# Attention with two MoE layers on one core: the reciprocal of the row sums goes from VectorE to GpSimd, as a power of -1

## The chip, the core and the metric

The kernel runs on one core of a Trainium2 chip. The core has TensorE (matrix products, PE in the profile; its weight loads are PEld), VectorE (DVE), ScalarE (ACT), GpSimd (POOL) and SyncE (SP, which here starts the transfers). The engines run their own lists of instructions in order and wait for each other at semaphores. The metric is the device time of one execution in microseconds, the lower the better.

## The reference

The input is q, k and v of 4 batches, 8 heads, 576 positions and 64 numbers a head. The attention drops the scores that lie more than tau under the maximum of their row:

```python
scores = scale * np.matmul(q, k.transpose(0, 1, 3, 2))
thresh = np.max(scores, axis=-1, keepdims=True) - tau
scores = np.where(scores >= thresh, scores, -1000000000.0)
scores = scores - np.max(scores, axis=-1, keepdims=True)
attn = np.exp(scores)
attn = attn / (np.sum(attn, axis=-1, keepdims=True) + 1e-09)
return np.matmul(attn, v).astype(np.float32)
```

Its output, 2304 tokens of 512 numbers, goes through a first MoE, `(relu(x @ w_in) ** 2) @ w_out` with 2048 inner units, and then a second one: each token picks the expert with the largest of 8 gate logits, goes through `relu(x @ w1[e]) @ w2[e]` and is scaled by a gate.

## The kernel before

Two heads make a pair; a batch has 4 pairs, all batches together 16. Each pair has 9 chunks of 128 rows of queries (the last rows of both heads share a chunk), 144 chunks in all, 36 a batch. For a chunk these steps follow each other, with the line of each:

- TensorE makes the scores of 128 rows and 576 keys in PSUM (L612; L648 for the first four chunks).
- VectorE takes the negated maximum of a row (L615).
- ScalarE makes the exponential (L618), and meanwhile GpSimd the row's threshold (L623).
- VectorE zeroes what lies under the threshold and adds up the row (L627, "mask"; a second record reads the accumulated sum).
- GpSimd adds 1e-9 to the sum (L632), VectorE takes the reciprocal (L635).
- The row is scaled by it, "norm": on GpSimd (L638), for the first head of each pair in the first batch on ScalarE (L671).
- TensorE turns the 128 x 576 probabilities in five transposes (L680) into the one PSUM buffer that there is for it, and ScalarE copies them out (L688).

When a group of chunks is through, TensorE multiplies them with V (L707), and ScalarE and VectorE split the result in a high and a low part (L711, L714). The queries and keys of the next pair are split the same way ahead of time (L534 to L543). In the first batch there are three PSUM buffers for scores, shared with the product with V, and later two. Five buffers hold probabilities, four each the maxima, thresholds and sums.

As soon as a batch's attention is done, its first product of the first MoE (L771) runs between the chunks of the next batch; its weights are unpacked and split on ScalarE, VectorE and GpSimd (L746 to L756). After the attention come the second product (L889), the gate, and the second MoE's slots of tokens (L1155, L1205).

The order on each engine is made on the host before the kernel is built: every step is a task with an engine, an assumed duration and a priority; a list scheduler picks, engine by engine, the startable task with the smallest priority. A step's priority in the attention is the chunk's number plus an offset from the table `PLACE`, which has one number for the first batch and one for the others.

Of the kernel before, what the change touches and what calls it, by code (L numbers as in the profile page):

```python
# [9 lines left out]
F32 = mybir.dt.float32  # L10
# [5 lines left out]
ALU = mybir.AluOpType  # L16
# [199 lines left out]
def c_dve(n, rate=1):  # L216
    return n / 960 / rate + 0.068
# [40 lines left out]
def moa(ctx, tc, q, k, v, tau, w_in, w_out, wg, wog, w1, w2, ctab, coln, out):  # L258
    nc = tc.nc
    B, H, S, D = 4, 8, 576, 64  # L260
    P = 128
# [45 lines left out]
    const = ctx.enter_context(tc.tile_pool(name="const", bufs=1))  # L307
# [4 lines left out]
    g = Graph()  # L312


    PLACE = {
        "scores": (-9, -4),
        "max": (-16, 3),
        "exp": (4, -9),
        "bound": (-22, 3),
        "mask": (-11, -14),  # L320
        "sum": (-16, -13),
        "norm": (-3, 13),
        "turn": (-1, 8),
        "parts": (2, 9),
        "av": (2, 3),
        "prep": (6, 9),
        "x": (14, 11),
    }

    def K(nm, pr):  # L330
        return PLACE[nm][pr >= NP]
# [142 lines left out]
    nc.scalar.dma_start(taub, tau.rearrange("(o t) -> o t", o=1).broadcast_to([P, 1]))  # L474
    ntau = const.tile([P, 1], F32, name="ntau")
    nc.vector.tensor_scalar(ntau, taub, 0.0, -1.0, op0=ALU.max, op1=ALU.mult)
    qsc = const.tile([P, 1], F32, name="qsc")
    nc.vector.tensor_scalar(qsc, taub, 0.0, 0.125, op0=ALU.is_ge, op1=ALU.mult)

# [9 lines left out]
    def new(nm, tag):  # L489
        return Buf(ALL[nm], f"{nm}{tag}")  # L490
# [100 lines left out]
    def t_chunk(n, key):  # L591
        pr, st = divmod(n, NST)
# [3 lines left out]
        nm, th, sm = (new(x, n) for x in ("nm", "th", "sm"))  # L596
# [31 lines left out]
                p3, s.t[:, :, :HALF], th.t, p3, op0=ALU.is_ge, op1=ALU.mult, accum_out=sm.t  # L628
            )

        def r1():
            nc.gpsimd.tensor_scalar(sm.t, sm.t, 1.0, 1e-9, op0=ALU.mult, op1=ALU.add)  # L632

        def r2():
            nc.vector.reciprocal(sm.t, sm.t)  # L635

        def nrm():
            nc.gpsimd.tensor_scalar(p.t[:, :S], p.t[:, :S], sm.t, 1.0, op0=ALU.mult, op1=ALU.mult)  # L638
# [25 lines left out]
        g.add("ACT", c_act(S, True, 1), ex, [s, nm], [p], key + K("exp", pr))  # L664
        g.add("POOL", 0.2, thr, [nm], [th], key + K("bound", pr))
        g.add("DVE", c_dve(S) + 0.085, msk, [s, th], [p, sm], key + K("mask", pr))
        g.add("POOL", 0.2, r1, [], [sm], key + K("sum", pr))
        g.add("DVE", 0.09, r2, [], [sm], key + K("sum", pr))
        if pr < NP and hd == 0:
            g.add("ACT", c_act(S, False, 1),  # L670
                  lambda: nc.scalar.activation(p.t[:, :S], p.t[:, :S], AF.Copy, scale=sm.t), [sm], [p],  # L671
# [565 lines left out]
    for pr in range(NPR):  # L1237
        b, hp = divmod(pr, NP)
        if pr + 1 < NPR:
            pair_prep(pr + 1, (pr * NST + K("prep", pr)) * T0)  # L1240
        for st in range(NST):
            n = pr * NST + st
            t_chunk(n, n * T0)
            if st in READY:
                t_av(pr, READY[st], (n + K("av", pr)) * T0)
        if hp == NP - 1:
            if b == 1:
                for i in range(NFC):
                    t_w(i, wkey[i])
                for u in range(2 * NFC):  # L1250
                    t_h(0, u // 2, u % 2, (NP * NST + 8 + u * 1.125) * T0)
            for u in range(2 * NFC) if b else ():
                t_h(b, u // 2, u % 2, ((b + 1) * NP * NST + 8 + u * (1.125 if b < B - 1 else 0.25)) * T0)
# [109 lines left out]
```

## Time and profile before

| | us |
|---|---|
| median of 3 timed runs | 985.02 (983.87 to 986.71) |
| profiled execution | 990.66 |
| its span, first to last instruction | 988.9 |
| TensorE busy | 957.8 (97%) |
| VectorE busy | 613.1 (62%) |
| ScalarE busy | 595.5 (60%) |
| GpSimd busy | 278.8 (28%) |

The profiled execution is one run with the profiler on. Busy shares are averages over stages that differ: the attention of the first batch up to about 100 us, the attention of the other three with the first product of the first MoE between it up to about 430 us, and the rest. Columns of the views are named where they first stand. A record of a matmul is longer than the time to the next one, because they overlap. A wait is put down to the instruction that released it last by the profile: where the table names a reciprocal as what ScalarE or GpSimd waited for, it is often the instruction just before it that they need.

### The profile page before, as it was taken

How to read it: one execution, taken by the hardware profiler on the slowest of the kernel's cores; microseconds unless marked ns; L12 is line 12 of the kernel's file. 1: busy time of each engine (PE TensorE's matmuls, PEld its weight loads, DVE VectorE, ACT ScalarE, POOL GpSimd, SP SyncE). 2: the span in 40 equal slices, each digit the busy share in tenths (PEclk: the TensorE clock that was granted, in tenths of full speed). 3: DMA queues.
4: the chain of work that ended last, by engine and by line, in shares of the span. 5: the costliest groups of instructions: out<-in, count | busy, mean ns of one | idle time of the engine just before them, and what ended most of it. 6: DMA issues, size and time to landing. Idle time of an engine off the chain costs nothing. (4 is left out here: it accounts for less than half of the span.)

```text
span 988.9 us, 18351 instructions
## 1 busy us (share of the span) xinstructions
PE 957.8 (97%) x6194; PEld 829.9 (84%) x6194; DVE 613.1 (62%) x1414; ACT 595.5 (60%) x1122; POOL 278.8 (28%) x511
## 2 busy tenths in 40 slices
PE   8888999999999999999999999999999999999996
PEld 7665888898889888989988888887889989889885
DVE  6786898775666565657613444445877667777730
ACT  5787777776666665665324444444647667876731
POOL 3343676663343434410001000001114210211200
PEclk7998999999999999999999999999999999999999
DMA  6566758665555542469713444445949767877700
GB/s 161 143 166 171 205 165 236 185 177 146 148 135 149 131 116 82 128 196 281 219 55 108 107 107 107 107 107 131 265 128 334 263 219 265 299 263 252 269 21 25
DMA packets 130569, 167.42 MB, mean 169 GB/s; under 512 B 21279, under 2 KB 87327, under 8 KB 130466
## 3 DMA queue, kind: packets, MB, share of 16 engines
q1 hardware_dynamic: 126226, 155.63, 54.1%
q0 software_dynamic: 4096, 10.52, 3.4%
q8 instruction: 51, 0.84, 0.4%
q14 instruction: 52, 0.43, 0.2%
q10 hardware_dynamic: 144, 0.00, 0.0%
HBM read 110.33 MB, written 29.56 MB: 141 GB/s over the span
## 5 line engine op out<-in xcount | busy, mean ns | idle before, releaser
L889 PE MATMUL banks<-w,memr 128*128 128x512 f32 x648 | 158.4, 395 | 0.0
L627 DVE SCALAR_TENSOR_TENSOR memf<-banks,memf 128x576 f32<-128x576 f32 x144 | 116.1, 813 | 62.0 <-ACT memf L618 53.1
L771 PE MATMUL banks<-memr,w 128*128 128x288 f32 x960 | 140.9, 297 | 0.0
L618 ACT ACTIVATE memf<-banks,memf 128x576 f32<-128x576 f32 x144 | 105.6, 743 | 56.4 <-DVE memf L615 28.7
L889 PEld LDWEIGHTS banks<-w,memr 128*128 128x128 f32 x648 | 119.1, 188 | 23.8
L771 PEld LDWEIGHTS banks<-memr,w 128*128 128x128 f32 x960 | 130.8, 188 | 2.9 <-issue 2.9
L615 DVE TENSOR_REDUCE memf<-banks 128x1 f32<-128x576 f32 x144 | 107.1, 752 | 19.2 <-PE banks L612 14.5
L680 PE MATMUL banks<-ident,memf 128*128 128x128 f32 x720 | 105.8, 278 | 10.4 <-ACT pt L688 10.0
L612 PE MATMUL banks<-memr 128*128 128x288 f32 x592 | 110.2, 314 | 4.2 <-DVE memf L627 3.0
L688 ACT ACTIVATE pt<-banks 128x640 f32<-128x640 f32 (+1 forms) x160 | 102.7, 651 | 16.3 <-PE banks L680 12.0
L638 POOL TENSOR_SCALAR memf<-memf 128x576 f32<-128x576 f32 x128 | 103.7, 812 | 17.3 <-DVE memf L635 13.6
L680 PEld LDWEIGHTS banks<-ident,memf 128*128 128x128 f32 x720 | 83.9, 142 | 21.0 <-ACT pt L688 5.8
L994 POOL DMA_INDIRECT lst<-memf x18 | 18.7, 1039 | 273.6 <-DVE memf L980 209.3
L612 PEld LDWEIGHTS banks<-memr 128*128 128x128 f32 x592 | 84.1, 192 | 11.5 <-DVE memf L627 5.1
L707 PE MATMUL banks<-pt,memf 128*64 128x256 f32 (+1 forms) x640 | 89.3, 423 | 1.6 <-DVE memf L627 0.7
L874 DVE TENSOR_TENSOR memr<-memf,memr 128x512 fp32r<-128x512 f32 x72 | 47.7, 690 | 65.9 <-ACT memf L871 65.9
L1155 PE MATMUL banks<-memr,w 128*128 128x256 f32 x432 | 85.8, 284 | 2.0 <-DVE memr L1165 2.0
L1140 DVE TENSOR_TENSOR w<-memf,w 128x512 fp32r<-128x512 f32 x114 | 75.0, 688 | 20.2 <-ACT w L1137 19.0
L771 PE MATMUL banks<-memr 128*128 128x288 f32 x576 | 85.1, 297 | 0.0
L1155 PE MATMUL banks<-memr 128*128 128x256 f32 x432 | 84.9, 283 | 0.0
L771 PEld LDWEIGHTS banks<-memr 128*128 128x128 f32 x576 | 78.7, 188 | 2.0 <-issue 2.0
L707 PEld LDWEIGHTS banks<-pt,memf 128*64 128x64 f32 x640 | 46.1, 141 | 34.2 <-issue 6.0
(142 smaller groups left out, 1530.1 us busy)
## 6 DMA issues: line engine op xcount, KB each, us to landing
memf<-in_moe_w_dram SPq DMA_DIRECT2D x104, 512.0 KB, 5.2
r_scr<-memf SPq DMA_DIRECT2D x128, 144.0 KB, 2.8
memf<-r_scr SPq DMA_DIRECT2D x36, 512.0 KB, 5.1
memr<-memr SPq DMA_DIRECT2D x64, 144.0 KB, 2.5
memr<-memr SPq DMA_DIRECT2D x64, 128.0 KB, 3.4
memr<-memr SPq DMA_DIRECT2D x32, 256.0 KB, 3.6
memf<-in_moe_w_in_dram SPq DMA_DIRECT2D x16, 512.0 KB, 5.1
memf<-in_moe_w_out_dram SPq DMA_DIRECT2D x16, 512.0 KB, 4.8
```

What stands on the lines that cost most here:

```text
L612: nc.tensor.matmul(s.t[:, hf, :HALF], qo, ko[:, halves[hf]], start=(i == 0), stop=(i == len(ops) - 1))
L615: nc.vector.tensor_reduce(nm.t, s.t[:, :, :HALF], axis=AX.XY, op=ALU.max, negate=True)
L618: nc.scalar.activation(p.t[:, :S].rearrange("p (a n) -> p a n", a=2), s.t[:, :, :HALF], AF.Exp, bias=nm.t)
L627: nc.vector.scalar_tensor_tensor(p3, s.t[:, :, :HALF], th.t, p3, op0=ALU.is_ge, op1=ALU.mult, accum_out=sm.t)
L638: nc.gpsimd.tensor_scalar(p.t[:, :S], p.t[:, :S], sm.t, 1.0, op0=ALU.mult, op1=ALU.mult)
L680: nc.tensor.transpose(ps.t[:, j], p.t[:, j * P : (j + 1) * P], ident)
L688: lambda pt=pt, j=j, c0=c0, w=w, off=off: nc.scalar.activation(pt.t[:, j, :, off : off + w], ps.t[:, :, c0 : c0 + w], AF.Copy),
L707: nc.tensor.matmul(out(slice(64 * j, 64 * j + 64)), raw.t[:, j, c], pt.t[:, j, c, :N], start=(c == 0), stop=(c == NQ - 1))
L771: nc.tensor.matmul(ps.t[:, :HALF], wv[:, a, kc], xT.t[:, x, kc, half], start=(i == 0), stop=(i == len(seq) - 1),)
L889: nc.tensor.matmul(ps.t, s.t[:, fc], wob[fc].t[:, x], start=(fc == 0 and i == 0), stop=(fc == NFC - 1 and i == 2))
L1140: lambda i=i, w=w, raw=raw: nc.vector.tensor_tensor(w.t[:, 1], raw.t[:, i], w.t[:, 0].bitcast(F32), op=ALU.subtract),
L1155: nc.tensor.matmul(ps.t[:, :256], w1b[kc][fc // 4].t[:, a, (fc % 4) * P : (fc % 4 + 1) * P], x2.t[:, x, kc], start=(i == 0), stop=(i == 11))
```

## The change

The addition of 1e-9 stays on GpSimd. The reciprocal becomes a second GpSimd instruction behind it, a two-tensor operation with a column of -1 as exponent; VectorE fills that column once at the start. The list scheduler is told of a GpSimd task of 0.3 us in place of a VectorE task of 0.09 us, and 19 of the 24 numbers of `PLACE` are other ones. The reciprocal in the gate (L988) stays.

```diff
     PLACE = {
-        "scores": (-9, -4),
-        "max": (-16, 3),
-        "exp": (4, -9),
...
+        "scores": (-9, -2),
+        "max": (-17, 4),
+        "exp": (7, -10),
...
+    neg1 = const.tile([P, 1], F32, name="neg1")
+    nc.vector.memset(neg1, -1.0)
...
+        def r0():
+            nc.gpsimd.tensor_scalar(sm.t, sm.t, 1.0, 1e-9, op0=ALU.mult, op1=ALU.add)
+
         def r1():
-            nc.gpsimd.tensor_scalar(sm.t, sm.t, 1.0, 1e-9, op0=ALU.mult, op1=ALU.add)
-
-        def r2():
-            nc.vector.reciprocal(sm.t, sm.t)
+            nc.gpsimd.tensor_tensor(sm.t, sm.t, neg1, op=ALU.pow)
...
-        g.add("POOL", 0.2, r1, [], [sm], key + K("sum", pr))
-        g.add("DVE", 0.09, r2, [], [sm], key + K("sum", pr))
+        g.add("POOL", 0.2, r0, [], [sm], key + K("sum", pr))
+        g.add("POOL", 0.3, r1, [], [sm], key + K("sum", pr))
```

Lines of the changed kernel are two higher than before from the new memset on. VectorE at the end of the first batch, before: the last maxima (L615), masks (L627) and reciprocals (L635) of the batch, then the split of the product with V (L714); L748, L750 and L752 unpack weights.

```order
L627 SCALAR_TENSOR_TENSOR memf<-banks,memf 128x576
L615 TENSOR_REDUCE memf<-banks 128x1
L635 RECIPROCAL memf<-memf 128x1
L627 SCALAR_TENSOR_TENSOR memf<-banks,memf 128x576
L748 TENSOR_SCALAR memf<-memf 128x512
L627 SCALAR_TENSOR_TENSOR memf<-banks,memf 128x576
L635 RECIPROCAL memf<-memf 128x1
L750 SCALAR_TENSOR_TENSOR memf<-memf 128x512
L635 RECIPROCAL memf<-memf 128x1
L714 TENSOR_TENSOR memr<-banks,memr 128x256
```

The same place on VectorE in the changed kernel (masks are L629, maxima L617; L750, L752 and L754 unpack weights):

```order
L629 SCALAR_TENSOR_TENSOR memf<-banks,memf 128x576
L617 TENSOR_REDUCE memf<-banks 128x1
L629 SCALAR_TENSOR_TENSOR memf<-banks,memf 128x576
L617 TENSOR_REDUCE memf<-banks 128x1
L750 TENSOR_SCALAR memf<-memf 128x512
L752 SCALAR_TENSOR_TENSOR memf<-memf 128x512
L629 SCALAR_TENSOR_TENSOR memf<-banks,memf 128x576 x2
L754 SCALAR_TENSOR_TENSOR memf<-memf 128x512
L543 TENSOR_TENSOR memr<-memf,memr 128x576
L716 TENSOR_TENSOR memr<-banks,memr 128x256
```

The reciprocals are gone, the last two masks of the batch come behind two steps of unpacking, and one step of the next pair's keys (L543) has come ahead of the product with V.

GpSimd at the same place, before (L623 threshold, L632 addition, L638 norm, L756 the split of a weight):

```order
L623 TENSOR_SCALAR memf<-memf,ntau 128x1
L638 TENSOR_SCALAR memf<-memf 128x576
L632 TENSOR_SCALAR memf<-memf 128x1 x2
L638 TENSOR_SCALAR memf<-memf 128x576 x2
L756 TENSOR_TENSOR memr<-memf,memr 128x512 x2
```

GpSimd there in the changed kernel (L625 threshold, L634 addition, L637 power, L640 norm):

```order
L625 TENSOR_SCALAR memf<-memf,ntau 128x1
L640 TENSOR_SCALAR memf<-memf 128x576
L634 TENSOR_SCALAR memf<-memf 128x1
L637 TENSOR_TENSOR memf<-memf,neg_97 128x1
L634 TENSOR_SCALAR memf<-memf 128x1
L640 TENSOR_SCALAR memf<-memf 128x576
L637 TENSOR_TENSOR memf<-memf,neg_97 128x1
L640 TENSOR_SCALAR memf<-memf 128x576
L758 TENSOR_TENSOR memr<-memf,memr 128x512 x2
```

Each addition has a power behind it in GpSimd's own list, and the last norm of the batch stands behind a power.

TensorE in the second pair of the first batch, before (L612 scores, L680 transposes, L707 product with V):

```order
L707 MATMUL banks<-pt_82,memf 64x256 x10
L680 MATMUL banks<-ident,memf 128x128 x5
L612 MATMUL banks<-memr 128x288 x8
L680 MATMUL banks<-ident,memf 128x128 x5
L612 MATMUL banks<-memr 128x288 x4
L680 MATMUL banks<-ident,memf 128x128 x5
L612 MATMUL banks<-memr 128x288 x8
L680 MATMUL banks<-ident,memf 128x128 x5
L612 MATMUL banks<-memr 128x288 x4
L680 MATMUL banks<-ident,memf 128x128 x5
L707 MATMUL banks<-pt_83,memf 64x320 x10
```

TensorE there in the changed kernel (L614, L682 and L709):

```order
L709 MATMUL banks<-pt_82,memf 64x256 x10
L682 MATMUL banks<-ident,memf 128x128 x5
L614 MATMUL banks<-memr 128x288 x12
L682 MATMUL banks<-ident,memf 128x128 x15
L709 MATMUL banks<-pt_83,memf 64x320 x10
```

Scores of three chunks are made at once, and the turns of three chunks follow each other with nothing between them.

## Rows read from the trace of the kernel before

**Rows 1.** Stages: us, busy PE, PEld, DVE, ACT, POOL (records), PEclk, DMA, GB/s

```profile
0.00:100.00 100.00, 84.67 (x535) 64.82 (x536) 72.74 (x175) 71.98 (x117) 38.47 (x111) 0.90 0.62 159
100.00:430.00 330.00, 327.00 (x2522) 292.08 (x2523) 227.74 (x526) 220.51 (x393) 170.14 (x339) 1.00 0.56 154
```

**Rows 2.** Waits: total us, times, longest; to 100 us, second row 100 to 430

```profile
PE banks L680 <- ACT pt L688: 10.0, 16, 1.2
...
PE banks L612 <- DVE memf L627: 2.0, 4, 1.2
...
DVE memf L635 <- POOL memf L632: 1.1, 4, 0.3
```

**Rows 3.** Groups by line: busy us, mean ns, idle before, releasers

```profile
L635 DVE RECIPROCAL memf<-memf 128x1 f32<-128x1 f32 x144 | 22.5, 157 | 8.8 <-POOL memf L632 6.9
...
L632 POOL TENSOR_SCALAR memf<-memf 128x1 f32<-128x1 f32 x144 | 35.0, 243 | 93.4 <-DVE memf L627 75.7 <-DVE memf L635 15.6
...
L756 POOL TENSOR_TENSOR w<-memf,w 128x512 fp32r<-128x512 f32 x10 | 13.5, 1346 | 4.4 <-ACT w L753 3.3 <-DVE memr L541 0.7
...
L756 DVE TENSOR_TENSOR w<-memf,w 128x512 fp32r<-128x512 f32 x12 | 8.2, 686 | 0.6 <-ACT w L753 0.5
```

**Rows 4.** Stage to 100 us, records of L635 alone: DVE busy (count)

```profile
0.00:100.00 100.00, 5.63 (x36) 0.90 0.62 159
```

**Rows 5.** Timeline from 45 us: start us, us, instruction, idle before, releaser

```profile
45.27 0.19 POOL L632 TENSOR_SCALAR memf<-memf 128x1 f32<-128x1 f32 x1 [0.77 <-DVE memf L627]
45.34 0.76 DVE L615 TENSOR_REDUCE memf<-banks 128x1 f32<-128x576 f32 x1 [0.16 <-PE banks L612]
...
46.01 0.15 DVE L635 RECIPROCAL memf<-memf 128x1 f32<-128x1 f32 x1
46.08 0.80 DVE L627 SCALAR_TENSOR_TENSOR memf<-banks,memf 128x576 f32<-128x576 f32 x1
...
46.48 0.77 ACT L671 ACTIVATE memf<-memf 128x576 f32<-128x576 f32 x1
...
46.98 0.19 POOL L632 TENSOR_SCALAR memf<-memf 128x1 f32<-128x1 f32 x1 [0.44 <-DVE memf L627]
...
47.20 0.16 DVE L635 RECIPROCAL memf<-memf 128x1 f32<-128x1 f32 x1 [0.31 <-POOL memf L632]
47.57 0.75 POOL L638 TENSOR_SCALAR memf<-memf 128x576 f32<-128x576 f32 x1 [0.40 <-DVE memf L635]
```

**Rows 6.** Timeline from 82.9 us, one chunk's addition and the next chunk's mask

```profile
82.94 0.19 POOL L632 TENSOR_SCALAR memf<-memf 128x1 f32<-128x1 f32 x1 [0.37 <-DVE memf L627]
...
83.69 0.27 POOL L623 TENSOR_SCALAR memf<-memf,ntau 128x1 f32<-128x1 f32 x1 [0.56 <-DVE memf L635]
83.82 0.76 ACT L618 ACTIVATE memf<-banks,memf 128x576 f32<-128x576 f32 x1
...
84.97 0.80 DVE L627 SCALAR_TENSOR_TENSOR memf<-banks,memf 128x576 f32<-128x576 f32 x1
```

**Rows 7.** Timeline of TensorE: products with V, first L771; then three stages

```profile
25.89 4.01 PE L707 MATMUL banks<-pt,memf 128*64 128x256 f32 x20 [0.73 <-DVE memf L627]
...
45.78 2.38 PE L707 MATMUL banks<-pt,memf 128*64 128x256 f32 x20
...
75.78 2.91 PE L707 MATMUL banks<-pt,memf 128*64 128x320 f32 x20
...
93.45 5.33 PE L707 MATMUL banks<-pt,memf 128*64 128x320 f32 x20
...
100.46 2.81 PE L771 MATMUL banks<-memr 128*128 128x288 f32 x20
...
33.00:38.00 5.00, 3.03 (x22) 2.59 (x23) 4.53 (x12) 4.71 (x8) 1.42 (x7) 1.00 0.21 81
87.00:91.00 4.00, 2.17 (x17) 1.68 (x15) 2.41 (x7) 2.37 (x5) 2.73 (x4) 0.96 0.76 158
90.00:98.00 8.00, 6.78 (x28) 4.86 (x29) 2.39 (x4) 3.91 (x7) 1.37 (x2) 0.57 0.76 239
```

More of the change, by code (lines that the diff above doesn't have):

```diff
@@ L315, in moa @@
     PLACE = {
-        "scores": (-9, -4),
-        "max": (-16, 3),
-        "exp": (4, -9),
[L319 to L327, printed above, removed]
+        "scores": (-9, -2),
+        "max": (-17, 4),
+        "exp": (7, -10),
+        "bound": (-21, 3),
+        "mask": (-11, -17),
+        "sum": (-17, -14),
+        "norm": (-2, 15),
+        "turn": (1, 7),
+        "parts": (-2, 11),
+        "av": (2, 2),
+        "prep": (1, 9),
+        "x": (13, 4),
     }
```

## The prediction

> **What bounds the kernel now.** I read the table of stages first, then the list of waits, then the timeline of a few microseconds. The stages [rows 1] split the kernel into two unlike parts. From 100 us on, TensorE is the bound: it is busy 327.0 of 330 us up to 430, and its idle time there is four kinds of wait whose sum is 3.1 us, the longest being 2.0 us for the masks of L627 to free a score buffer [rows 2]. In this stretch the matmuls of the first MoE (L771) fill what the attention leaves open. Before 100 us there is nothing to fill with: the first batch's attention runs alone. Up to 100 us TensorE is busy 84.7, VectorE 72.7, ScalarE 72.0, GpSimd 38.5 [rows 1], and TensorE waits 10.0 us for the copies of turned probabilities (L688), because there is one buffer for transposes. Three engines of similar load wait for each other there, so a shorter queue on one of them gives back a part of its length, not the whole. VectorE's own wait at the reciprocal is 1.1 us in four cases there [rows 2].
>
> After the attention, the order of instructions on every engine is the same in both kernels: the last 4188 of 6906 instructions on TensorE, the last 862 on VectorE, the last 108 on GpSimd stand in the same order. So the change can act only up to about 430 us, and in practice on when the first batch's attention ends (first matmul of L771 at 100.46 us [rows 7]): behind that TensorE has its list of work and hardly waits. What is won or lost before 100 us is carried to the end one for one.
>
> **The change part by part.** *Removed from VectorE:* 144 reciprocals of 157 ns [rows 3], of which 36 fall before 100 us [rows 4]. Their place in the queue is shorter than their record: the maximum starts at 45.34, the reciprocal at 46.01, the mask at 46.08 [rows 5], so one holds up the next instruction by 0.07 us. 36 x 0.07 = 2.5 us; with the full record it would be 36 x 0.157 = 5.7 us, with VectorE never last it would be nothing. To that comes the head-of-line wait for GpSimd's addition, 1.1 us in four cases [rows 2]. Together 3.6 us, between 0 and 6.8. Since ScalarE is as busy as VectorE in the stretch and TensorE waits for ScalarE, I take half: 1.8 us. The other 108 reciprocals (108 x 0.07 = 7.6 us) lie in the stretch where TensorE is the bound; I cost them at nothing, and the cover is the 327 of 330 us of TensorE.
>
> *Added to GpSimd:* 144 powers of one column, each behind the addition and waiting for it. No row shows a power. From below it is bounded by an addition of one column, 243 ns on average [rows 3] and 0.19 us in the timeline [rows 5]; from above by GpSimd's subtraction of 512 columns with two tensors, 1346 ns [rows 3]. I take 0.3 us, nearest to the addition and to the threshold, 0.27 us [rows 6], which have the same size. GpSimd then gets 36 x 0.3 = 10.8 us more up to 100 us on top of 38.5: it has room. In the stretch up to 430 it gets 108 x 0.3 = 32 us on top of 170.1 of 330 [rows 1]. Cost: nothing, as long as nothing queued behind waits for it. What is queued behind is the next chunk's threshold (L623), for which VectorE's mask waits. In a typical chunk the addition starts at 82.94 and ends at 83.13, the threshold is at 83.69, the exponential starts at 83.82 and takes 0.76, and the mask comes at 84.97 [rows 6]. A power from 83.23 on may last until about 84.31 before the mask, which waits for the exponential to 84.58 anyway, sees the threshold late: 1.08 us of slack against 0.3.
>
> The Trainium skill speaks against this placing: its page "GPSIMD Engine Reference", section "Engine selection", says that elementwise work belongs on VectorE, GpSimd being some two times slower for two inputs. This case's trace agrees for wide tiles: the same subtraction takes 1346 ns on GpSimd and 686 ns on VectorE [rows 3]. By that ratio, an estimate, the power would take 0.31 us in place of VectorE's 0.157, and the sum would stay as it is; the page says nothing of a power, whose work per element may be more.
>
> *The hop:* before, the sum's way to the normalisation is addition, VectorE, then GpSimd or ScalarE. Where VectorE is busy, the reciprocal waits behind a maximum: addition over at 45.46, reciprocal 46.01, normalisation 46.48, that is 1.02 us; where it is free: 47.17, 47.20, 47.57, that is 0.40 us [rows 5]. After: about 0.1 for the wait, 0.3 for the power, 0.1 to start: 0.5 us. Some chunks win half a microsecond and some lose a tenth. Transposes before 100 us wait for the copy of the chunk ahead and not for the normalisation [rows 2], so I cost it at nothing; were it the last wait in each of the 36 chunks, it would be between -0.5 x 36 and +0.1 x 36 of single waits, most of which overlap.
>
> *Moved:* 19 of the 24 priorities were changed with it. At the end of the first batch the last two masks now stand behind two steps of weight splitting (L748 and L750 of before) instead of between them. The same four transposes in a row on TensorE, each waiting for the copy of the one ahead, follow in both; these set the drain, and I cost the move at nothing. In the second pair of heads TensorE now has twelve score matmuls and then three transposes in a row, where scores and transposes took turns. That is the place that I trust least (below). One memset of a column on VectorE at the start is nothing.
>
> **Sum.** The profiled execution took 990.66 us (span 988.9); minus 1.8 gives 988.9, or 0.18%. It stands 0.6% above the median of the three timed runs, 985.02, so the forecast on that scale is 983.2. A measurement of this kernel can tell about 0.3% from no change, 3 us.
>
> **Rivals.**
> 1. VectorE is the engine that sets the first batch's pace, the relief comes in full (3.6 us), and the other order also removes the low clock at 26 to 29 us. For it: VectorE and ScalarE are the busiest there after TensorE, and the power hides. Against: TensorE's waits name ScalarE. The second of the clock's drops is the priced one: the product with V of 20 matmuls took 4.01 us at 25.89 against 2.38 at 45.78 at the full clock [rows 7], 1.6 us. Time: 985.0 - 3.6 - 1.6 = 979.8.
> 2. The stretch from 100 to 430 us isn't filled, and the other reciprocals count too: 985.0 - 1.8 - 7.6 = 975.6. Beside it stands a rule of the Trainium skill, page "Perfetto Trace Analysis", section "Identifying the Most-Contended Engine": a busy matmul row is no measure of headroom, the weight loads' share is. The loads are 292.1 of 330 us in that stretch [rows 1], which leaves 38 us by that rule. Against it: waits of only 3.1 us, where a late engine would have to show as a wait of TensorE.
> 3. Slower: the power is long. The place is GpSimd's queue in the first batch, the point is 1.08 us, where the threshold queued behind it becomes what the mask waits for. At 1.35 us, the upper row, it is about 0.27 us late in each of 36 chunks, 10 us, and GpSimd would be busy 38.5 + 36 x 1.35 = 87 of 100 us. Time: 985.0 - 1.8 + 10 = 993. For it: a power is no simple operation and has no row. Against: one column per row is little work even at a high cost per element.
> 4. The three transposes in a row leave TensorE so little busy that its clock falls to 1.2 GHz there. It did so behind the four in a row: busy 2.17 of 4 us from 87 to 91, then a granted clock of 0.57 on average from 90 to 98, and the product with V took 5.33 us where it takes 2.91 [rows 7], 2.4 us, plus some 0.8 us for two slowed transposes. A stretch of 3.03 of 5 us from 33 to 38 kept the full clock [rows 7]. Price 3.2 us: 986.4 with the forecast's gain, 988.2 without.
>
> That the reciprocals do not go away can be excluded: the new order has 144 powers and, up to the gate, no reciprocal on VectorE.
>
> **How the numbers follow.** Forecast 0.36, rival 1 0.33, rival 2 0.05, rival 3 0.14, rival 4 0.12 (half of it with the gain, half without). Faster by over 0.3%: rivals 1 and 2, 0.38. Within: forecast and half of rival 4, 0.42. Slower: rival 3 and the other half, 0.20. The forecast's own range is 981 to 986. The range for 8 in 10 goes down to 976.5 (the full records, 6.8 us, and the 1.6 us of clock) and up to 990, which takes in rival 4 and a power a little past its point, and leaves out the long power.
>
> **What would show it.** The power's duration on GpSimd: under 1.08 us supports the sum. The first matmul of L771: some 2 us earlier than 100.46 by the forecast, 5 by rival 1, later by rival 3; the end of the span moves by the same amount. Waits of VectorE's mask for GpSimd's threshold in the first 100 us: few by the forecast, one a chunk by rival 3. A granted clock of half between 40 and 60 us is rival 4. If the first matmul of L771 moves and the end does not, the claim that TensorE carries it through is wrong.

## The result: 0.96% slower

| | before | after |
|---|---|---|
| median of 6 timed runs each, us | 984.44 (980.36 to 986.71) | 993.40 (991.72 to 995.12) |
| ratio, with its 95% interval | | 1.0096 [1.0072, 1.0119] |
| profiled execution, us | 990.66 | 993.49 |
| its span, us | 988.9 | 991.7 |

The timed difference is +9.0 us, the difference of the two profiled executions only +2.8: the profile of before is of an execution 6 us over its own median. A second profile of before took 985.51 us, span 983.7; it is the one compared below. Lines after the added memset are two higher after: L773 is the first product, L682 the turns, L690 their copies, L709 the product with V, L625 the threshold, L629 the mask, L634 the addition, L637 the power, L758 the weight split.

Stages of after, columns as in [rows 1], with 100 to 200 us apart:

```profile
0.00:100.00 100.00, 83.39 (x521) 63.65 (x523) 71.18 (x139) 71.58 (x115) 59.10 (x147) 0.95 0.64 165
100.00:430.00 330.00, 324.34 (x2496) 288.15 (x2493) 217.85 (x413) 218.85 (x386) 222.43 (x439) 1.00 0.53 150
100.00:200.00 100.00, 95.39 (x720) 82.42 (x718) 77.97 (x147) 70.48 (x127) 81.42 (x143) 1.00 0.66 184
```

The same view of the second profile of before:

```profile
100.00:200.00 100.00, 98.02 (x753) 86.37 (x752) 85.68 (x195) 75.75 (x138) 71.63 (x119) 1.00 0.75 206
```

From 100 to 430 us GpSimd (the last busy time ahead of the clock) is busy 52.3 us more than in [rows 1], and TensorE 2.7 us less. The place is the first 100 us of that stretch: GpSimd was busy 71.63 of 100 there before the change, not the 52% of the whole stretch, and 81.42 after; TensorE gets 720 matmuls through in place of 753, though a part of that gap is only that the second batch starts later (below).

Groups of GpSimd after, columns as in [rows 3]:

```profile
L637 POOL TENSOR_TENSOR memf<-memf,neg 128x1 f32<-128x1 f32 x144 | 83.2, 579 | 10.7
...
L634 POOL TENSOR_SCALAR memf<-memf 128x1 f32<-128x1 f32 x144 | 36.5, 254 | 95.7 <-DVE memf L629 91.3 <-DVE memf L837 0.9
```

Single lines of after (shortest, median and longest ns; first and last start in us): the power, and the first product of the first MoE, which stands for the first row of L771 in [rows 7]:

```profile
L637 POOL TENSOR_TENSOR memf<-memf,neg x144: 543/548/1126, 12.6 to 435.1; 128x1 f32<-128x1 f32 x144
...
L773 PE MATMUL banks<-memr x576: 288/295/401, 103.5 to 468.0; 128*128 128x288 f32 x192
```

The power takes 548 ns, against 157 for the reciprocal [rows 3]. The first product starts at 103.5 us; in the second profile of before it starts at 98.1:

```profile
L771 PE MATMUL banks<-memr x576: 288/295/406, 98.1 to 459.3; 128*128 128x288 f32 x192
```

Waits of after, columns as in [rows 2]: the first three rows up to 100 us, the others from 100 to 430:

```profile
PE banks L682 <- ACT pt L690: 9.5, 13, 1.5
...
ACT memf L673 <- POOL memf L637: 3.8, 6, 1.7
...
DVE memf L629 <- POOL memf L625: 1.9, 3, 0.7
...
PE banks L614 <- DVE memf L629: 3.2, 6, 1.1
...
DVE memf L629 <- POOL memf L625: 51.1, 52, 1.4
```

The last row is new in size against before. In the second profile of before, VectorE's mask waits for GpSimd's threshold only so much from 100 to 430 us:

```profile
DVE memf L627 <- POOL memf L623: 8.4, 13, 1.7
```

But the size of this row does not measure the loss. The run e2 below has the new order with the reciprocal on VectorE, no power at all, and loses nothing in this stretch; its row from 100 to 430 us is:

```profile
DVE memf L629 <- POOL memf L625: 40.1, 43, 1.2
```

So most of the 51.1 us comes with the new order, and it lies behind 200 us, where it costs nothing. What goes with the loss is the part from 100 to 200 us; the same wait there in after, in the second profile of before and in e2:

```profile
DVE memf L629 <- POOL memf L625: 9.6, 14, 1.4
...
DVE memf L627 <- POOL memf L623: 6.4, 10, 1.7
...
DVE memf L629 <- POOL memf L625: 2.5, 7, 1.2
```

TensorE sees a late mask where it frees a score buffer late (3.2 us in six cases, above).

How one of those waits comes about, timeline of after (start, us, instruction, idle before, releaser):

```profile
131.94 0.75 POOL L637 TENSOR_TENSOR memf<-memf,neg 128x1 f32<-128x1 f32 x1
132.46 1.35 POOL L758 TENSOR_TENSOR memr<-memf,memr 128x512 fp32r<-128x512 f32 x1
132.57 0.75 DVE L617 TENSOR_REDUCE memf<-banks 128x1 f32<-128x576 f32 x1
...
133.42 0.74 ACT L620 ACTIVATE memf<-banks,memf 128x576 f32<-128x576 f32 x1 [0.75 <-DVE memf L617]
...
133.90 0.51 POOL L634 TENSOR_SCALAR memf<-memf 128x1 f32<-128x1 f32 x1
...
134.51 1.18 POOL L640 TENSOR_SCALAR memf<-memf 128x576 f32<-128x576 f32 x1
...
135.67 0.54 POOL L637 TENSOR_TENSOR memf<-memf,neg 128x1 f32<-128x1 f32 x1
...
135.75 0.77 PE L682 MATMUL banks<-ident,memf 128*128 128x128 f32 x5 [0.48 <-POOL memf L640]
...
136.21 0.26 POOL L625 TENSOR_SCALAR memf<-memf,ntau 128x1 f32<-128x1 f32 x1
...
136.51 0.82 DVE L629 SCALAR_TENSOR_TENSOR memf<-banks,memf 128x576 f32<-128x576 f32 x1 [1.42 <-POOL memf L625]
...
137.39 0.79 PE L614 MATMUL banks<-memr 128*128 128x288 f32 x4 [0.34 <-DVE memf L629]
```

The maximum is there at 133.32 and the exponential at 134.16. The threshold, 0.26 us of work, stands on GpSimd behind a power, a weight split, an addition, a normalisation and another power, and comes at 136.21. The mask starts 1.42 us late, and the scores at 137.39 stand 0.34 us for the buffer that it frees; the turn at 135.75 had stood 0.48 us for the normalisation in the same queue. This is the queue that the prediction looked at only in a chunk of the first batch [rows 6], where no split stands in it.

### Where the 8 us between two profiles lie

The kernel falls into three parts: up to the first matmul of the first product (t1), from there to the first matmul of the second product (L889, L891 after), and the rest to the span's end.

| profile | t1, us | t1 to second product | rest |
|---|---|---|---|
| before, first profile | 100.5 | 394.1 | 494.3 |
| before, second profile | 98.1 | 393.1 | 492.5 |
| after | 103.5 | 396.5 | 491.7 |
| after, second profile | 99.3 | 396.8 | 491.7 |

After against the second profile of before: 5.4 + 3.4 - 0.8 = 8.0 us, the difference of the spans. The middle part agrees between the two profiles of after, t1 does not (103.5 and 99.3): of these 4.2 us, 2.8 are there when TensorE's first turn starts (15.6 and 12.8 us). That varies from run to run of one kernel, so single profiles size the middle part well and the first part badly.

Where in the middle part the time goes shows when matmuls are counted from each profile's own t1. In the first 100 us TensorE gets 755 through in the second profile of before, 728 in after and 763 in e2; it waits 1.7, 4.2 and 1.1 us there, and the mask waits 5.7, 9.6 and 2.5 us for the threshold. In the next 200 us the counts are 1549, 1554 and 1559. The 27 matmuls that after lacks, at 100/755 us each, are 3.6 us (an estimate), about what its middle part is longer.

### The profile page after: what moved, and what is told of

Read it like the earlier page. It is cut to its first block, busy times and chain, and to the rows that moved or that the text cites. A ratio compares the mean times of both kernels' runs of the same rounds, so it can differ in the third digit from the quotient of the medians.

```text
span 991.7 us, 18300 instructions
## 1 busy us (share of the span) xinstructions
PE 959.6 (97%) x6194; PEld 830.1 (84%) x6194; DVE 605.1 (61%) x1271; ACT 597.8 (60%) x1122; POOL 354.1 (36%) x655
## 5 line engine op out<-in xcount | busy, mean ns | idle before, releaser
L629 DVE SCALAR_TENSOR_TENSOR memf<-banks,memf 128x576 f32<-128x576 f32 x144 | 116.9, 817 | 94.8 <-POOL memf L625 54.1
L891 PE MATMUL banks<-w,memr 128*128 128x512 f32 x648 | 159.4, 396 | 0.0
L773 PE MATMUL banks<-memr,w 128*128 128x288 f32 x960 | 140.4, 296 | 0.8 <-DVE memr L716 0.8
L891 PEld LDWEIGHTS banks<-w,memr 128*128 128x128 f32 x648 | 119.1, 188 | 24.6
L773 PEld LDWEIGHTS banks<-memr,w 128*128 128x128 f32 x960 | 130.9, 188 | 3.5 <-issue 2.4
L682 PE MATMUL banks<-ident,memf 128*128 128x128 f32 x720 | 106.2, 279 | 14.6 <-ACT pt L690 9.9
L617 DVE TENSOR_REDUCE memf<-banks 128x1 f32<-128x576 f32 x144 | 107.7, 754 | 16.2 <-PE banks L614 12.2
L614 PE MATMUL banks<-memr 128*128 128x288 f32 x592 | 110.9, 314 | 5.2 <-DVE memf L629 3.7
L690 ACT ACTIVATE pt<-banks 128x640 f32<-128x640 f32 (+1 forms) x160 | 102.4, 651 | 20.0 <-PE banks L682 15.9
L682 PEld LDWEIGHTS banks<-ident,memf 128*128 128x128 f32 x720 | 83.2, 142 | 30.2 <-POOL memf L634 6.2
L640 POOL TENSOR_SCALAR memf<-memf 128x576 f32<-128x576 f32 x128 | 103.0, 805 | 9.2
L614 PEld LDWEIGHTS banks<-memr 128*128 128x128 f32 x592 | 83.7, 191 | 10.8 <-DVE memf L629 7.0
L709 PE MATMUL banks<-pt,memf 128*64 128x256 f32 (+1 forms) x640 | 88.7, 423 | 0.0
L637 POOL TENSOR_TENSOR memf<-memf,neg 128x1 f32<-128x1 f32 x144 | 83.2, 579 | 10.7
L773 PE MATMUL banks<-memr 128*128 128x288 f32 x576 | 85.2, 296 | 0.0
L1142 DVE TENSOR_TENSOR w<-memf,w 128x512 fp32r<-128x512 f32 x114 | 74.8, 687 | 14.1 <-ACT w L1139 10.8
L773 PEld LDWEIGHTS banks<-memr 128*128 128x128 f32 x576 | 78.9, 188 | 0.8 <-issue 0.8
```

The source lines that it names most:

```text
L614: nc.tensor.matmul(s.t[:, hf, :HALF], qo, ko[:, halves[hf]], start=(i == 0), stop=(i == len(ops) - 1))
L617: nc.vector.tensor_reduce(nm.t, s.t[:, :, :HALF], axis=AX.XY, op=ALU.max, negate=True)
L629: nc.vector.scalar_tensor_tensor(p3, s.t[:, :, :HALF], th.t, p3, op0=ALU.is_ge, op1=ALU.mult, accum_out=sm.t)
L637: nc.gpsimd.tensor_tensor(sm.t, sm.t, neg1, op=ALU.pow)
L682: nc.tensor.transpose(ps.t[:, j], p.t[:, j * P : (j + 1) * P], ident)
L690: lambda pt=pt, j=j, c0=c0, w=w, off=off: nc.scalar.activation(pt.t[:, j, :, off : off + w], ps.t[:, :, c0 : c0 + w], AF.Copy),
```

## The experiments

All ratios are to the kernel before on the same chip, with 95% intervals. Two things were changed at once: where the reciprocal is made, and `PLACE`. The kernels below mix them, and by batches. In the table "old" and "new" are `PLACE` of before and of after.

| | reciprocals | powers in first batch only | powers in later batches only | powers |
|---|---|---|---|---|
| old | 1 | e10: 1.0000 [0.9982, 1.0019] | e11: 1.0041 [1.0027, 1.0055] | e1: 1.0014 [1.0001, 1.0027] |
| first column old, second new | e9: 0.9988 [0.9978, 0.9997] | e12: 1.0012 [1.0001, 1.0023] | | e7: 1.0043 [1.0026, 1.0059] |
| new | e2: 1.0012 [0.9999, 1.0025] | e13: 1.0036 [1.0018, 1.0055] | e14: 1.0073 [1.0051, 1.0094] | after: 1.0096; e8: 1.0116 [1.0094, 1.0138] |

The scheduler is told of VectorE's 0.09 us in the kernels e0, e1, e9 to e12 and e16 and of GpSimd's 0.3 us in the others (0.65 in e5), whatever is issued.

### Power and order apart: e0, e1, e2, e3

**e0** is the kernel before, unchanged, with a profile.

> The unchanged kernel, profiled once more. Its first profile (990.66 us) is 6 us above the median of its timed runs, 984.4, and shows a granted clock of half from about 9 to 19 us; the changed kernel's profile (993.49, its median) has full clock there. If that early drop is a matter of chance and explains the 6 us, this profile has full clock up to 20 us and some 984 us, and its first matmul of L771 comes some 5 us earlier, near 95 us instead of 100.5. If the drop belongs to the order of before, it is there again and the time is near 990.

It took 985.51 us. Its granted clock was 1.00 from 8 to 20 us, where the first profile's was 0.57, so that drop does not belong to the order; the first product came 2.4 us earlier, not 5. Its other rows stand above.

**e1**: the old order with powers.

```diff
-            nc.vector.reciprocal(sm.t, sm.t)
+            nc.gpsimd.tensor_tensor(sm.t, sm.t, neg1, op=ALU.pow)
```

> Power on GpSimd, but every engine in the order of before: the priorities and assumed durations of before, the power stands in GpSimd's list where the reciprocal stood in the common order. Theory A (the power is long: 0.55 us against the 0.3 of the forecast, and what stands behind it on GpSimd comes late): slower than before by most of the 9 us, 5 to 9. Theory B (the new order is the cause, with its three turns in a row and the low clock behind them): within 3 us of before.

**e2**: the new order, told of the same tasks, with the reciprocal issued on VectorE.

```diff
-            nc.gpsimd.tensor_tensor(sm.t, sm.t, neg1, op=ALU.pow)
+            nc.vector.reciprocal(sm.t, sm.t)
```

> The order of the changed kernel on every engine, but the reciprocal is VectorE's again, where the power stood in the common order. Theory A (long power): near before, within 3 us. Theory B (order): slower by 5 to 9 us, with the granted clock at half near 55 to 62 us as in the changed kernel.

**e3**: the new order with a multiplication in place of the power. The sums are left out of the scaling: every row is scaled by 0.1875 squared, and other tokens go to the experts.

```diff
-    nc.vector.memset(neg1, -1.0)
+    nc.vector.memset(neg1, 0.1875)
...
-            nc.gpsimd.tensor_tensor(sm.t, sm.t, neg1, op=ALU.pow)
+            nc.gpsimd.tensor_tensor(sm.t, neg1, neg1, op=ALU.mult)
```

> The changed kernel, with a short two-tensor product of constant columns on GpSimd in the place of each power; the sums are left out of the scaling (a constant factor stands for the reciprocal). Theory A: the 9 us come back, time within 3 us of before or below it. Theory B: still slower by 5 to 9 us, low clock near 55 us.

Measured: e1 987.39 us (ratio 1.0014), e2 986.82 (1.0012). Each half costs little; both together cost 1.0096. Theory A failed in e1 and theory B in e2: neither the power alone nor the order alone makes the result. e3 took 1061.96 us, because the second MoE got more slots, so its total says nothing; up to the second product its trace can be read. Its middle part is 390.7 us and e2's 391.6, against 396.5 of after. So the new order would run the middle part *faster* than before does (393.1), if the instruction on GpSimd were short (a median of 194 ns in e3, 548 for the power) or were not there; what costs 5 us there is the power's length (e3's instruction doesn't read the sum either, but stands in the same queue), not that GpSimd has one more instruction.

### Which part of GpSimd's queue: e5, e6

**e5**: after, with the scheduler told 0.65 us for the power, somewhat more than the 0.548 measured.

```diff
-        g.add("POOL", 0.3, r1, [], [sm], key + K("sum", pr))
+        g.add("POOL", 0.65, r1, [], [sm], key + K("sum", pr))
```

> The changed kernel, with the list scheduler told 0.65 us for the power in place of 0.3 (its record is 0.55 us, and 0.54 to the next start), same priorities. Theory C (the order is made for a power half as long as it is, so the places behind it come late): 4 to 8 us faster than the changed kernel, that is 985 to 989. Theory D (GpSimd has too little room from 100 to 200 us for any order with powers, and the first batch's priorities cost the rest): at most 3 us faster, 990 to 993, with GpSimd busy 40 of 50 us or more from 100 to 150.

**e6**: after, with the third kind of weight split always on VectorE, at the same place in the order.

```diff
-              lambda: rest[2].tensor_tensor(w.t[:, 1], av.t, w.t[:, 0].bitcast(F32), op=ALU.subtract),
+              lambda: nc.vector.tensor_tensor(w.t[:, 1], av.t, w.t[:, 0].bitcast(F32), op=ALU.subtract),
```

> The changed kernel in its own order, but the 16 subtractions of the weight splitting that GpSimd makes between 90 and 210 us (1.35 us each, 21 us) are done by VectorE at the same place (0.69 us each). Theory D: TensorE's work from 100 to 200 us comes back, 3 to 5 us faster than the changed kernel (988 to 990), the time from the first matmul of L773 to the first of L891 falls from 396.5 to some 392; the first batch stays late (103 us). Theory C: within 2 us of the changed kernel, 991 to 995, or slower, since VectorE gets 11 us more.

Measured: e5 989.83 us, 1.0060 [1.0044, 1.0076], against 1.0116 of the unchanged kernel in the same set (e8, below). With the longer duration the scheduler makes another order, and between a third and a half of the loss is gone; e5's middle part is 394.7. e6: 991.13 us (988.07 to 997.77), 1.0089 [1.0061, 1.0118]: the total decides nothing. Its middle part is 393.4, 3.1 us less than after, and its stage from 100 to 200 us reads:

```profile
100.00:200.00 100.00, 97.71 (x745) 85.48 (x744) 88.47 (x167) 74.01 (x134) 76.28 (x137) 1.00 0.68 190
```

Without these splits GpSimd is busy 76.28 in place of 81.42, and TensorE does 745 matmuls in place of 720. So the splits are part of the queue that makes the powers dear; no run takes the splits away with reciprocals in place, so how much of the 3.1 us belongs to the powers is not shown. The groups of GpSimd in the second profile of before, from 100 to 200 us, show how much they hold already there:

```profile
L756 POOL TENSOR_TENSOR w<-memf,w 128x512 fp32r<-128x512 f32 x8 | 11.4, 1429 | 1.8 <-DVE memf L615 0.8 <-ACT w L753 0.7
...
L756 POOL TENSOR_TENSOR memr<-memf,memr 128x512 fp32r<-128x512 f32 x4 | 5.3, 1318 | 0.2 <-ACT memr L753 0.2
```

16.7 of the 71.63 us are splits. The 32 powers of after in these 100 us add 20.2 us:

```profile
L637 POOL TENSOR_TENSOR memf<-memf,neg 128x1 f32<-128x1 f32 x32 | 20.2, 634 | 2.0
```

### Which column of PLACE: e7, e8

**e7**: after, with the first batch's column of before (the nine numbers that differ; three of them here). **e8** is after, unchanged.

```diff
-        "max": (-17, 4),
-        "exp": (7, -10),
+        "max": (-16, 4),
+        "exp": (4, -10),
...
-        "prep": (1, 9),
+        "prep": (6, 9),
```

> The changed kernel, with the first batch's column of priorities taken from before (twelve numbers) and the other batches' column left as changed. TensorE's order in the first batch is then that of before, without three turns in a row. Theory D (two places: the first batch's order, 3 to 5 us, and GpSimd from 100 to 200 us, 3 to 4 us): 3 to 5 us faster than the changed kernel, 988 to 990; first matmul of L773 at 97 to 99 us instead of 103.5. If the first batch's order is no cause: 992 to 994.

> The changed kernel once more, timed beside the other three on the same chip: 993 by its first runs, ratio 1.009 to before. Its profile tells which of its stages repeat: by theory D the first matmul of L773 is near 103 us again, and the stretch from there to the first of L891 near 396 us.

Measured: e7 988.06 us, 1.0043 [1.0026, 1.0059]; e8 995.99 us, 1.0116 [1.0094, 1.0138]. The first column costs 5.2 us against the result above and 7.2 against e8. The profiled executions of after and e7 lie at their medians, and between them the loss lies before t1, as the single lines of e7 show:

```profile
L773 PE MATMUL banks<-memr x576: 288/294/403, 95.7 to 462.2; 128*128 128x288 f32 x192
```

95.7 against 103.5 us (99.3 in e8, whose profiled execution is 6.4 us under its median). Its middle part stays long, 398.4.

### By batches: e9 to e14

**e10** and **e11**: old order, powers in the first batch (`pr < NP`) or in the later ones (`pr >= NP`). **e13** and **e14**: the same in the new order.

```diff
-            nc.vector.reciprocal(sm.t, sm.t)
+            if pr < NP:
+                nc.gpsimd.tensor_tensor(sm.t, sm.t, neg1, op=ALU.pow)
+            else:
+                nc.vector.reciprocal(sm.t, sm.t)
```

> Before in its own order, with powers on GpSimd in the first batch alone (36) and VectorE's reciprocals in the others (108). If the forecast's step for the first batch holds (VectorE's queue is relieved and GpSimd has room there): 1 to 3 us faster than before, 981.5 to 983.5. If powers don't help there either: within 1 us of before or slower.

> Before in its own order, with VectorE's reciprocals in the first batch and powers on GpSimd in the other three (108). Theory D (GpSimd is full from 100 to 200 us, its thresholds and norms come late, masks free their score buffers late, TensorE waits): 2 to 4 us slower than before, with the time from the first matmul of the first MoE to the first of the second product at 396 to 398 us against 393 to 394. If TensorE hides them, as forecast: within 1 us.

> The changed kernel in its own order, powers on GpSimd in the first batch alone, reciprocals on VectorE (at the powers' places) in the others. If the later powers cost 4 us in this order too, and the first batch's column costs most with powers behind it: 988 to 990, 4 us faster than the changed kernel and 3 to 5 slower than before. If the first batch's powers don't matter in this order: near 986, as with all reciprocals in it.

> The changed kernel in its own order, reciprocals on VectorE in the first batch, powers on GpSimd in the other three. If the two costs are separate: 986 (new order with reciprocals) + 4 = 990. If the cost of the new column comes from powers of the first batch alone: 988 to 989.

**e9**: before, with the second column of after (shown in part); **e12**: e9 with powers in the first batch.

```diff
-        "mask": (-11, -14),
-        "sum": (-16, -13),
-        "norm": (-3, 13),
+        "mask": (-11, -17),
+        "sum": (-16, -14),
+        "norm": (-3, 15),
```

> Before, with the first batch's priorities of before and the new ones for the other three batches, reciprocals on VectorE. With both columns new and reciprocals it was 1.2 us slower than before, the first batch some 4 us longer and the stretch from the first MoE's first matmul to the second product 1.5 us shorter. If the two columns act separately: 1 to 2.5 us faster than before. If the shorter stretch was chance: within 1 us.

> The same priorities as in the run with both columns from different kernels (first batch old, others new), powers on GpSimd in the first batch alone, reciprocals on VectorE in the others. If the two gains are real and add up: 2 to 4 us faster than before, 980 to 982. If neither is: within 1 us of before.

Measured: e10 984.54 us, e11 988.92, e13 988.50, e14 991.47, e9 983.80, e12 985.58; ratios in the table. The later powers cost 0.41% in the old order and 0.61% in the new one (e14 less e2), 4 and 6 us; the first batch's powers nothing in the old order (interval -1.8 to 1.9 us of loss) and 0.24% in the new one (e13 less e2). With the first column old and the second new they cost 0.24% too (e12 less e9, on one chip), so the 980 to 982 us expected of e12, if the two gains added up, were missed. In the new order the parts add up to the whole: 0.12 + 0.24 + 0.61 = 0.97%, measured 0.96% (1.16% in e8); the sum is known to some 0.3%.

The middle parts say the same without any timing. With powers in the later batches they are 396.6 (e1), 396.7 (e11), 398.4 (e7), 396.5 (after), 396.8 (e8) and 396.9 (e14 and e15) us, 394.7 where the scheduler is told 0.65 (e5); with reciprocals 394.1 and 393.1 (before), 392.7 (e10), 393.8 (e9), 394.2 (e12), 391.6 (e2), 391.5 (e13) and 391.8 (e16). e11 is the later powers alone, without any of the new numbers, and shows the same stage as after (stages, then waits from 100 to 200 us):

```profile
100.00:200.00 100.00, 96.14 (x733) 84.06 (x732) 81.68 (x156) 72.98 (x131) 85.94 (x150) 1.00 0.72 198
```

```profile
PE banks L614 <- DVE memf L629: 3.4, 5, 1.2
```

In the second profile of before that wait is there too, but short:

```profile
PE banks L612 <- DVE memf L627: 1.1, 4, 0.4
```

e9 is the only kernel that comes out ahead of before, by 0.12% [0.03%, 0.22%]: reciprocals where they were, and the new second column.

### The clock in the first batch: e15, e16

In after, three turns in a row from 53.65 us wait for the copies, and the granted clock falls. Timeline, then windows of after (columns as in [rows 1]):

```profile
48.15 2.38 PE L709 MATMUL banks<-pt,memf 128*64 128x256 f32 x20
...
53.65 0.74 PE L682 MATMUL banks<-ident,memf 128*128 128x128 f32 x5 [0.83 <-POOL memf L625]
...
55.48 1.04 PE L682 MATMUL banks<-ident,memf 128*128 128x128 f32 x5 [1.09 <-ACT pt L690]
...
57.32 1.33 PE L682 MATMUL banks<-ident,memf 128*128 128x128 f32 x5 [0.80 <-ACT pt L690]
...
58.58 4.88 PE L709 MATMUL banks<-pt,memf 128*64 128x320 f32 x20
...
69.28 2.38 PE L709 MATMUL banks<-pt,memf 128*64 128x256 f32 x20
```

```profile
54.00:58.00 4.00, 2.11 (x12) 1.50 (x11) 2.33 (x5) 4.00 (x8) 0.48 (x3) 0.72 0.43 101
58.00:63.00 5.00, 5.00 (x22) 2.35 (x22) 1.55 (x4) 2.01 (x3) 3.43 (x7) 0.54 0.93 215
```

From the third product with V to the fifth it takes 69.28 - 48.15 = 21.1 us (20.3 in e8). e2 and e14 both have reciprocals in the first batch and run the same instructions there. In e2's profile the granted clock falls at this place (0.81 from 54 to 63 us), in e14's it is 1.00. First e2, then e14:

```profile
47.95 2.38 PE L709 MATMUL banks<-pt,memf 128*64 128x256 f32 x20
...
56.56 4.54 PE L709 MATMUL banks<-pt,memf 128*64 128x320 f32 x20
...
66.92 2.38 PE L709 MATMUL banks<-pt,memf 128*64 128x256 f32 x20
```

```profile
46.60 2.38 PE L712 MATMUL banks<-pt,memf 128*64 128x256 f32 x20
...
55.20 2.91 PE L712 MATMUL banks<-pt,memf 128*64 128x320 f32 x20
...
63.92 2.38 PE L712 MATMUL banks<-pt,memf 128*64 128x256 f32 x20
```

That is 19.0 and 17.3 us, and the difference is the product's, 4.54 against 2.91: the low clock cost 1.6 us here. With powers and the low clock the stretch is 1.3 us (e8) to 2.2 us (after) longer than in e2. In e3, the short instruction in the same order, the clock stayed up and it is 17.3 us too.

**e15** keeps TensorE busy there: six turns whose result nobody reads, behind the turns of chunks 14 to 17. **e16** does it in e9, for `n in (6, 7, 8) or 32 <= n <= 35`.

```diff
+            for j in range(6 if 14 <= n <= 17 else 0):
+                nc.tensor.transpose(psum[:, 5 * 512 + 256 : 5 * 512 + 384], ident, ident)
```

> The changed kernel, with six idle transposes of the identity into an unused part of the same PSUM bank behind each of four turns in the second pair, where three turns stand in a row; they run while TensorE waits for ScalarE's copy. If the granted clock falls at 55 us because TensorE has too little to do there, it stays full until the drain near 93 us, the next product with V takes 2.9 us instead of 4.6 to 4.9, and the time is 1.5 to 3 us under the changed kernel. If the drop has another cause, it is there as before.

> The fastest version so far (first batch's priorities of before, the others' new, reciprocals on VectorE), with the same six idle transposes behind the turns at the end of the first pair and at the end of the first batch, where the clock fell at 26 and at 90 us in the profiles with a drop. If they keep the clock up: 1 to 3 us faster than that version, 981 to 983. If the turns' copies are what sets the drain, whatever the clock: within 1 us of it.

Measured: e15 993.41 us, 1.0094 [1.0076, 1.0111]; e16 987.71 us, 1.0028 [1.0013, 1.0043] against 0.9988 for e9. The clock stayed up, as timeline and windows of e15 show:

```profile
46.24 2.38 PE L711 MATMUL banks<-pt,memf 128*64 128x256 f32 x20
...
53.65 0.74 PE L682 MATMUL banks<-ident,memf 128*128 128x128 f32 x5 [0.89 <-ACT pt L692]
54.23 0.82 PE L684 MATMUL banks<-ident 128*128 128x128 f32 x6
...
55.84 0.76 PE L682 MATMUL banks<-ident,memf 128*128 128x128 f32 x5 [0.79 <-ACT pt L692]
56.53 2.91 PE L711 MATMUL banks<-pt,memf 128*64 128x320 f32 x20
...
65.61 2.38 PE L711 MATMUL banks<-pt,memf 128*64 128x256 f32 x20
```

```profile
54.00:58.00 4.00, 3.21 (x27) 2.17 (x27) 3.05 (x7) 3.36 (x6) 1.67 (x4) 1.00 0.85 191
```

The same product took 4.88, 4.60 and 4.94 us in the profiles of after, e8 and e6, which have no added turns. In this stretch the filler won time: 65.61 - 46.24 = 19.4 us against 21.1, though the turns stood 2.2 us apart where after has 1.8, since ScalarE's copy is released behind the added turns too. The whole kernel shows no gain (993.41 us against 993.40 and, in e8, 995.99). In e16's profile the granted clock is 1.00 from 24 to 32 and from 84 to 104 us, where e9's is 0.79 and 0.83, and the kernel is slower than e9. So both expectations of a gain failed, though the clock stayed up in both profiles; why the added turns cost what they won is not shown.

## Why the prediction was wrong

The forecast of 983.2 us is missed by 10.2 us, and 993.4 lies outside its range.

**The step that failed first** stands under *Added to GpSimd*: "In the stretch up to 430 it gets 108 x 0.3 = 32 us on top of 170.1 of 330 [rows 1]. Cost: nothing, as long as nothing queued behind waits for it." These 108 powers cost 4 us in the old order (e11) and 6 in the new (e14 less e2), the greatest of the three terms that make up the loss in the new order. GpSimd's room was taken from a mean over 330 us, though 12 of its 16 weight splits lie in the first 100 us of that stretch, where GpSimd stood at 71.6. There the condition "nothing queued behind waits for it" was false: the mask already waited 6.4 us for the threshold before, and 9.6 us in after and 14.1 in e11. And TensorE's 327 of 330 us, which the prediction names as cover for the 108 reciprocals taken away, did not mean that it had no time to lose: the middle part ran between 390.7 and 398.4 us. The Trainium skill's rule behind rival 2 (page "Perfetto Trace Analysis", section "Identifying the Most-Contended Engine": go by the weight loads' share, not the matmuls') was right that a row of busy matmuls hides slack. Of the 38 us that it would leave, the runs show 2.4 that could be won (393.1 to 390.7, e3), and more that could be lost.

**Rival 3 was the right mechanism in the wrong place.** It had the late threshold, with the point 1.08 us, in the first batch. The power took 0.548 us, below that point, and in the old order the first batch lost nothing that shows (e10). The same threshold was late in the second batch, where 1.35 us splits and the normalisation share the queue. Its 993 us came from 36 delays in the first batch, which no run shows, so the agreement with 993.4 is an accident.

**The size of the power** was taken as 0.3 us from the addition; measured 0.548, inside the bounds of 0.19 and 1.346. By the working 0.55 still looked free, so the right size alone would not have turned the forecast. In the runs the size decides: with 0.194 us in the same places the middle part lost nothing (390.7, e3), with 0.548 it lost 5 us; no run shows whether 0.3 would have been free. The ratio to the reciprocal is 548/157 = 3.5, where the estimate by the Trainium skill's page "GPSIMD Engine Reference", section "Engine selection", had used the two that the page gives for add, mul and max; the direction agrees, the size does not for this operation. The scheduler was told 0.3 as well; told 0.65 (e5) the kernel is 3.5 us under the result above and 5.5 under e8.

**"Moved: I cost the move at nothing" failed too.** With powers the first column costs 5 to 7 us (after and e8 against e7), with reciprocals 2.4 (e2 against e9, told of different tasks). The place "that I trust least" was where it shows: three turns in a row, 2.11 of 4 us busy, then a granted clock of 0.54, 1.2 GHz for most of these 5 us, and a product with V of 4.88 us in place of 2.91. That is rival 4's sign, and e2 beside e14 prices it at 1.6 us. Rival 4's own 2.4 us set the batch's last product beside one from its middle; at a granted clock of 1.00 the last one took 3.77 us (L707 at 92.69 in the second profile of before), so 1.6 of its 2.4 were the clock's. But the whole stretch, 21.1 us in after and 20.3 in e8, is 20.1 us in e7, so it holds 1.0 us or less of the 5 to 7. From the first turn to the third product after and e8 take 2.6 and 2.1 us more than e7, and from the fifth product to t1 1.7 us more. What makes these, and which of the nine numbers, stays open.

**The relief of VectorE, 1.8 us**, was not seen. e10 has the change between 1.8 us of gain and 1.9 of loss, so a gain of that size is compatible and not shown. Beside the new second column the powers in the first batch lost 0.24% (e12 less e9).

**What held.** What is late at the second product is late at the end: the rest is 490.3 to 494.8 us in all profiles but e3's. Up to 100 us the mask waits for the threshold 1.9 us in three cases, few, as the forecast had it. The hop shows as 3.8 us in which ScalarE's normalisation waits for the power, while TensorE's turns still wait for the copies above all, 9.5 us against 10.0 [rows 2].

**Still open:** powers in all batches cost less in the old order (e1, 0.14%) than those of the later batches alone (e11, 0.41%). The profiles have the same middle part (396.6 and 396.7), so what differs lies before t1, where a gain from the first batch's powers up to 2.7 us would explain it; e10 neither shows nor excludes 1.8 of that, and e12 beside e9 shows a loss instead. So what the powers of the first batch do depends on what else is in the kernel, and the account by batches is additive only in the new order.

## What to carry to other kernels

Read the room on an engine in the stretch where the new work lands, by 50 or 100 us, and look there at what stands behind it in that engine's queue; a mean over a long stage hides the part that is full. A short instruction on a side engine reaches TensorE by way of the buffer that the next waiting step frees, even where TensorE looks full: count its matmuls per stretch, not its busy time. The sum of an engine's waits is no price if that engine is not the bound: e2 has 40.1 us of the wait that looked guilty, and no loss. Where a host scheduler sets the order, its assumed duration is part of the change, and a table of priorities changed together with an operation has to be tested with the old operation and the new one apart.

## What the runs showed of the hardware

- A power of one column with a two-tensor operation on GpSimd takes 548 ns (543 to 1126); the addition of one column 254 on average, the reciprocal on VectorE 157.
- GpSimd's short instructions are longer in the full stretch: the power 634 ns on average from 100 to 200 us, and an addition of 0.51 us at 133.90, where 0.19 stands in [rows 5].
- The start of the first batch differs by 2.8 us between two executions of the same changed kernel (first turn at 15.6 and 12.8 us). 24 score matmuls ahead of it took 5.58 us in the one and 3.52 in the other.
- With turns added that nobody reads the granted clock was 1.00 from 54 to 58 us in one profile (e15), where it was 0.72 without them in after.
- The same instructions met the low clock in one execution (e2) and not in another (e14): a product with V of 20 matmuls took 4.54 us and 2.91 us.
